# Attention and two MLPs: seven of the eight layer-in products formed as Strassen's seven block products

## The chip, the cores and the metric

The kernel runs on one core of a Trainium2 chip. A time is the device time of one launch in microseconds (us), and a kernel's time is the median of several runs. A profile is one execution taken by the hardware profiler. Its engines are PE (TensorE, matmuls), DVE (VectorE), ACT (ScalarE), POOL (GpSimd) and SP (which starts the DMA transfers). PE's weight loads are listed apart as PEld.

## The reference, cut to what matters

```python
# 2 batches, 8 heads, 1152 positions, head_dim 64
q_pool = q.reshape(B, H, S // 2, 2, D).mean(axis=3)
scores = np.matmul(q_pool, k.transpose(0, 1, 3, 2)) / np.sqrt(D)
attn = softmax(scores)                        # over the keys
x = np.matmul(attn, v)                        # -> (1152 tokens, 512)
h = x @ moe_w_in;  x = np.maximum(0.01 * h, h) @ moe_w_out
h = x @ moe2_w_in; x = (h / (1 + np.exp(-h))) @ moe2_w_out
```

`w_in` is 512 x 2048 and `w_out` 2048 x 512. The inputs come as 64-bit floats, which the kernel reads as pairs of 32-bit words and turns into fp32 itself.

## The kernel before

The program has two parts, `attention` (to about 212 us in the trace) and `mlps`. The change works in the second, and in the attention only where the two meet.

**Precision.** PE multiplies in fp32r. To reach fp32 accuracy each operand is held as a high part (rounded to fp32r) and a low part (what is left), and each product takes three matmuls: high by high, high by low, low by high. The tokens are held as `xh` and `xl`, the weights as `w0h`, `w0l` (layer-in) and `w1h`, `w1l` (layer-out), and what lies between the two products as `gh` and `gl`.

**Blocks, groups and cells.** Each MLP (called a layer here) is done in four blocks of 512 hidden columns, so there are eight blocks. The 1152 tokens are two groups: group 0 is one stretch of 512, group 1 two stretches of 320. A unit is a layer, a block and a group. `layer_in` (L1102) makes 128 hidden rows of a unit: four steps over the 512 model columns (`kk`), three matmuls each, one per stretch of tokens (L1115). So 256 hidden rows take 24 matmuls of 512 columns for group 0 and 48 of 320 for group 1. Layer 1 then applies Prelu twice on ACT (to `gh`, L1141, and to the full value `a`, L1146), layer 2 a Sigmoid on ACT (L1153), a multiply on DVE out of PSUM (L1157) and a copy on ACT (L1162). POOL subtracts to get `gl` (L1168).

`layer_out_t` (L1172, layer 1) and `layer_out` (L1223, layer 2) form the second product (L1186, L1244) and add it up over the blocks in `acc1` or `acc2` (DVE, L1207 and L1263). The last block of layer 1 also writes the tokens of layer 2 (`xh` L1213 on ACT, `xl` L1218 on POOL). Two units stand interleaved, the layer-in of one with the layer-out of the one before.

**Weights.** A piece is 128 x 512 weights, eight to a block. It is loaded by a DMA (L135), converted from 64-bit words in five steps (`convert_steps`, L158): an absolute value on ACT (L171), then four on DVE (L175 clamp, L179 shift, L183 sign, L188 tail), all in the SBUF tile `wt`. Two more steps split it, high on ACT (L206) and low on POOL (L210). Three tiles receive raw pieces and four hold converted ones.

**PSUM.** `Banks` (L91) hands out the eight banks in four pairs, in turn.

**The last pair of heads.** The attention's last normalization runs inside `mlps`, while PE is at the first unit: two reciprocals (L826), two multiplies (L827), the high part on ACT (L828) and the low part on DVE (L829), 288 columns each. Group 1 of block 0 needs them for its fourth step over `kk`.

**The order.** `Plan` (L228) is a list scheduler that runs while the program is built. Each task has an engine, an assumed duration, a due time, tasks it follows and buffers it takes and gives back. Of the tasks that are ready on an engine the one due first is written next. What it writes is a fixed order for each engine; on the chip an instruction waits only by its semaphores, and all behind it on its engine wait too.

Of the kernel before, what the change touches and what calls it, by code (L numbers as in the profile page):

```python
# [1341 lines left out]
```

## Time and profile before

| | |
|---|---|
| median of 3 runs | 619.52 us (618.24 to 620.22) |
| the profiled execution | 620.76 us |
| its span, first to last instruction | 618.8 us |
| mean granted TensorE clock | 0.986 of full speed |
| PE busy | 606.9 us, 98% of the span |
| DVE, ACT, POOL busy | 462.0, 292.2, 316.4 us |
| idle before PE's layer-in matmuls | 0.0 us in all three of its groups |

A share of busy time is an average over stages. The chain that ended last is what shows, for each stretch, which engine the end waited for. A group of instructions gives the mean duration of one, and a timeline a single one with what it waited for in brackets. [...] Rows of the timeline with "x2" stand for two instructions, and the length is that of both.

### The profile page before, as it was taken

To read this page: it belongs to the slowest core of one execution; us is meant where nothing else is said; L and a number is where in the kernel's file an instruction comes from. 1 tells how busy PE (TensorE), PEld (TensorE's weight loads), DVE (VectorE), ACT (ScalarE), POOL (GpSimd) and SP (SyncE) were. 2 spreads that over 40 slices of the span, in tenths; PEclk is the share of its full clock that TensorE was granted. 3 is DMA by queue.
4 is the path that set the end of the run, shared out by engine and by line. 5 is a ranking of instruction groups with operands and counts; after the bars stand their busy time and mean duration, and the time that the engine had idled before them with its cause. 6 is when DMAs were issued, how large, how long until landed. Compare 5 with 4: busy or idle time off the path is not lost.

```text
span 618.8 us, 10706 instructions
## 1 busy us (share of the span) xinstructions
PE 606.9 (98%) x4244; PEld 511.0 (83%) x4244; DVE 462.0 (75%) x588; ACT 292.2 (47%) x501; POOL 316.4 (51%) x224
## 2 busy tenths in 40 slices
PE   7998999999999999999999999999999999999997
PEld 5867677686687698899899899999988988988986
DVE  6799897797898999666677656989898978752122
ACT  4556566576476464454243433554555443432210
POOL 7857558466461066355364355766665544433120
PEclk9598999999999999999999999999999999999999
DMA  7122442454131123323223223223143332200012
GB/s 256 51 78 61 114 139 59 114 174 160 21 113 56 55 61 109 137 62 100 94 87 93 87 93 103 88 83 103 69 127 106 107 96 77 68 1 0 1 52 102
DMA packets 29529, 55.01 MB, mean 89 GB/s; under 512 B 13196, under 2 KB 14632, under 8 KB 29480
## 3 DMA queue, kind: packets, MB, share of 16 engines
q1 hardware_dynamic: 29336, 54.14, 27.7%
q8 instruction: 33, 0.54, 0.4%
q10 hardware_dynamic: 144, 0.20, 0.1%
q14 instruction: 16, 0.13, 0.1%
HBM read 49.81 MB, written 2.42 MB: 84 GB/s over the span
## 4 chain that ended last, share of the span: by engine, by line
PE 61%; DVE 4%; issue 0%; ACT 0%; POOL 0%
PE psum L1115 29%; PE psum L1244 16%; PE psum L1186 16%; DVE acc L714 1%; DVE r L826 1%; DVE wt L183 1%; DVE wt L188 1%; DVE xl L845 1%; DVE wt L175 0%; DVE wt L179 0%; DVE pvs L841 0%; ACT xh L844 0%; POOL w1l L210 0%; DVE xl L829 0%; DVE pvs L827 0%
## 5 line engine op out<-in xcount | busy, mean ns | idle before, releaser
L1168 POOL TENSOR_TENSOR gl<-a,gh 128x512 fp32r<-128x512 f32 (+1 forms) x64 | 99.6, 1559 | 104.5 <-ACT gh L1162 50.9
L1115 PE MATMUL psum<-xh,w0h 128*128 128x320 f32 (+1 forms) x384 | 108.7, 337 | 0.0
L1115 PE MATMUL psum<-xh,w0l 128*128 128x320 f32 (+1 forms) x384 | 108.6, 337 | 0.0
L1115 PE MATMUL psum<-xl,w0h 128*128 128x320 f32 (+1 forms) x384 | 108.5, 337 | 0.0
L676 ACT ACTIVATE e<-psum 128x512 f32<-128x512 f32 (+1 forms) x144 | 88.6, 664 | 20.8 <-PE psum L670 18.3
L548 DVE TENSOR_REDUCE mx<-psum 128x2 f32<-128x768 f32 x96 | 88.2, 950 | 12.1 <-PE psum L541 10.9
L210 POOL TENSOR_TENSOR w0l<-wt,w0h 128x512 fp32r<-128x512 f32 x32 | 42.6, 1333 | 75.0 <-ACT w0h L206 71.9
L175 DVE TENSOR_SCALAR wt<-wt 128x512 f32<-128x512 f32 x64 | 50.2, 785 | 37.7 <-ACT wt L171 37.7
L1115 PEld LDWEIGHTS psum<-xh,w0h 128*128 128x128 f32 x384 | 67.7, 188 | 7.5 <-issue 0.9
L728 PE MATMUL psum<-e,vnat 128*64 128x320 f32 (+1 forms) x576 | 72.5, 408 | 0.1
L1115 PEld LDWEIGHTS psum<-xh,w0l 128*128 128x128 f32 x384 | 66.8, 188 | 5.7 <-POOL w0l L210 0.3
L1115 PEld LDWEIGHTS psum<-xl,w0h 128*128 128x128 f32 x384 | 66.8, 188 | 5.0
L210 POOL TENSOR_TENSOR w1l<-wt,w1h 128x512 fp32r<-128x512 f32 x32 | 44.7, 1395 | 38.1 <-ACT w1h L206 38.1
L179 DVE TENSOR_SCALAR wt<-wt 128x512 uint32<-128x512 uint32 x64 | 62.6, 979 | 1.6
L728 PEld LDWEIGHTS psum<-e,vnat 128*64 128x64 f32 x576 | 40.3, 137 | 28.3 <-ACT e L676 1.4
L714 DVE TENSOR_TENSOR acc<-acc,e 128x512 f32<-128x512 f32 (+1 forms) x77 | 62.5, 847 | 0.9
L183 DVE SCALAR_TENSOR_TENSOR wt<-wraw,wt 128x512 uint32<-128x512 uint32 x64 | 61.4, 960 | 1.6
L714 POOL TENSOR_TENSOR acc<-acc,e 128x512 f32<-128x512 f32 (+1 forms) x35 | 49.7, 1420 | 21.1 <-DVE acc L714 13.8
L188 DVE SCALAR_TENSOR_TENSOR wt<-wraw,wt 128x512 uint32<-128x512 uint32 x64 | 57.2, 893 | 1.8
L1244 PE MATMUL psum<-w1l,gh 128*128 128x512 f32 (+1 forms) x148 | 56.9, 385 | 0.0
L1244 PE MATMUL psum<-w1h,gh 128*128 128x512 f32 (+1 forms) x148 | 56.9, 385 | 0.0
L1244 PE MATMUL psum<-w1h,gl 128*128 128x512 f32 (+1 forms) x148 | 56.8, 384 | 0.0
(86 smaller groups left out, 1137.2 us busy)
## 6 DMA issues: line engine op xcount, KB each, us to landing
wraw<-in_moe_w_in_dram SPq DMA_DIRECT2D x32, 512.0 KB, 4.7
wraw<-in_moe_w_out_dram SPq DMA_DIRECT2D x32, 512.0 KB, 3.2
vnat<-in_v_dram SPq DMA_DIRECT2D x8, 576.0 KB, 6.5
knat<-in_k_dram SPq DMA_DIRECT2D x7, 576.0 KB, 6.2
qnat<-in_q_dram SPq DMA_DIRECT2D x7, 576.0 KB
out_dram<-acc SPq DMA_DIRECT2D x8, 256.0 KB, 2.0
xl<-pvs SPq DMA_DIRECT2D x7, 288.0 KB, 4.8
xh<-d SPq DMA_DIRECT2D x14, 144.0 KB, 2.9
```

Of the source, the lines that this page charges most:

```text
L179: nc.vector.tensor_scalar(out=t, in0=t, scalar1=4, scalar2=1, op0=ALU.logical_shift_left, op1=ALU.logical_shift_right)
L183: nc.vector.scalar_tensor_tensor(out=t, in0=box["high"], scalar=0x80000000, in1=t, op0=ALU.bitwise_and, op1=ALU.bitwise_or)
L188: nc.vector.scalar_tensor_tensor(out=box["out"], in0=box["low"], scalar=29, in1=box["t"], op0=ALU.logical_shift_right, op1=ALU.bitwise_or)
L210: self.nc.gpsimd.tensor_tensor(out=lo, in0=tf, in1=hi, op=ALU.subtract)
L548: nc.vector.tensor_reduce(out=mx[p][:, u, c], in_=ps[:, :, 0:KC], op=ALU.max, axis=AX.X)
L676: nc.scalar.activation(out=e_t[h, t], in_=ps[:, :, 0:n], func=ACTF.Exp, scale=scale)
L714: e.tensor_tensor(out=a, in0=e_t[h, 0] if t == 1 else a, in1=e_t[h, t], op=ALU.add)
L728: nc.tensor.matmul(out=vps[h][0][own[j], 0, 0:CW[c]], lhsT=vnat[p][:, j, t, :], rhs=e_t[h, t][:, j, :], start=(t == 0), stop=(t == NKT - 1),)
L1115: nc.tensor.matmul(out=box[x][:, c, 0:n], lhsT=wt[:, kk, fs], rhs=m[:, kk, chunk(g, c)], start=(kk == 0 and wt is wh and m is xh), stop=(k ...
L1168: nc.gpsimd.tensor_tensor(out=gl, in0=box["a", x], in1=gh, op=ALU.subtract)
L1186: nc.tensor.matmul(out=box[x][:, c, 0:n], lhsT=wt[:, f, ms], rhs=y[:, c * n:(c + 1) * n], start=(f == 0 and wt is oh and y is gh), stop=(f ...
L1244: nc.tensor.matmul(out=box[x][:, c, 0:n], lhsT=y[:, ts], rhs=wt[:, f, cs], start=(f == 0 and y is gh and wt is oh), stop=(f == FB - 1 and ...
```

## The change

Block 0 of layer 1 keeps its layer-in. For the other seven blocks the layer-in of 256 hidden rows and one group of tokens, a cell in what follows (28 of them), is taken as a product of 2 x 2 matrices of blocks: the 512 model columns in two halves, the 256 hidden rows in two halves of 128, the tokens of the group in two halves (256 or 320). Strassen's method, in Winograd's form, needs seven block products M1 to M7 instead of eight, each of 2 steps over `kk` by three matmuls: 42 matmuls of 256 or 320 columns.

It needs sums of the operands:

- *Tokens.* T1 to T4 are differences of token blocks, four subtractions on DVE for each layer and group (`transform`), each with a high part on ACT and a low part on POOL (the last two of layer 2's group 1 on DVE). For layer 1 the full tokens are first rebuilt from `xh` and `xl` on DVE (`rebuild`, L1207, four for each group).
- *Weights.* Each layer-in piece keeps three of its 128-column parts, copied by ACT, and gets four sums on DVE (`combine`). The split then runs over seven parts, 896 columns, instead of 512. Its DMA fetches two stretches of 512 words for each row instead of one of 1024.
- *Results.* The products of a cell lie in two PSUM pairs. ACT copies M1 out (e1), and DVE forms eu, ev, c1 and c2. M2 is written into M1's bank, M3 into M6's and M4 into M7's, so they follow e1, eu and ev. Prelu and Sigmoid then read SBUF.

The weight conversion of `mlps` runs in one PSUM pair that it keeps, one bank to a piece, and three pairs are left for matmuls. Raw pieces have two tiles instead of three, converted ones three instead of four. SiLU's multiply moves from DVE to POOL. A unit's layer-out now stands between its successor's two halves.

```diff
+    transform=10.0,
+    more=3.0,
     conv=4,
     early=3,
     early_due=60.21,
     split=4,
-    wt=4,
+    wt=3,
+    raw=2,
...
-        if kind == 0:
-            src = w[i * 128:(i + 1) * 128, 2 * fb * n:2 * (fb + 1) * n]
+        t = self.raw_p.tile([128, 2 * n], U32, tag="raw", name="wraw")
+        to = t
+        if kind == 1:
+            src = w[fb * n + i * 128:fb * n + (i + 1) * 128, :]
+        elif blk == 0:
+            src = w[i * 128:(i + 1) * 128, 0:2 * n]
         else:
-            src = w[fb * n + i * 128:fb * n + (i + 1) * 128, :]
-        t = self.raw_p.tile([128, src.shape[1]], U32, tag="raw", name="wraw")
-        self.nc.sync.dma_start(out=t, in_=src)
+            c = 2 * fb * n + (i // 2) * n
+            src = w[:, c:c + n].rearrange("(b k p) c -> k p b c", b=2, p=128)[i % 2]
+            to = t.rearrange("p (b c) -> p b c", b=2)
+        self.nc.sync.dma_start(out=to, in_=src)
...
+            if psum:
+                box["tf"] = psum(box["n"])
...
+        def copy():
+            new()
+            nc.scalar.activation(out=self.mid[box["n"]][:, 0:384], in_=box["tf"][:, 0:384], func=ACTF.Copy)
+        def sums():
+            self.combine(box["n"], box["tf"])
+        return (begin, clamp, shift, sign, tail) + ((copy, sums) if parts else ())
+    def combine(self, n, raw):
+        v = self.mid[n].rearrange("p (m f) -> p m f", f=128)
+        a12, _, a11, a21 = (raw[:, 128 * m:128 * (m + 1)] for m in range(4))
+        for to, x, y, op in (
+            (4, a21, v[:, 1], ALU.add), (5, v[:, 2], a21, ALU.subtract), (6, v[:, 4], a11, ALU.subtract), (3, a12, v[:, 6], ALU.subtract)
+        ):
+            self.nc.vector.tensor_tensor(out=v[:, to], in0=x, in1=y, op=op)
...
+            parts = [self.slots[self.SLOTS[i]][:, 896 * x:896 * (x + 1)] for x in range(2)]
+            self.tiles[blk, kind, i] = [x.rearrange("p (m f) -> p m f", f=128) for x in parts]
...
+    conv_ps, _ = banks.take()
...
+        if ph in (2 * NBLK - 1, 2 * NBLK):
+            order += outs + ins
+        elif ph == 2 * NBLK + 1:
+            order += ins + outs
+        else:
+            order += ins[0:1] + outs + ins[1:2]
...
+            steps = weights.convert_steps(lambda n: conv_ps[:, n % 2, :], kind == 0)
+            costs = ("ACT", 0.62), ("DVE", 0.62), ("DVE", 0.65), ("DVE", 0.65), ("DVE", 0.69), ("ACT", 0.5), ("DVE", 0.9)
+            into, last = (5, 6) if kind == 0 else (4, 4)
...
+        t1 = step(lo2(0), lo2(1), lo2(0), after, 0)
+        t3 = step(lo2(1), lo1(1), lo2(1), [t1], 2)
+        t2 = step(lo1(1), lo1(1), lo2(0), [t1, t3], 1)
+        t4 = step(lo1(0), lo1(0), lo1(1), [t2], 3)
...
+            fast = layer == 1 and g == 1 and m > 1
...
+    def rebuild(g, after):
+        made = []
+        for k in range(KDM):
+            made.append(add(
+                "DVE", 0.07 + 2 * groups[g][1] / 860, P["transform"] - 1.0 + 18.0 * g,
+                lambda k=k: nc.vector.tensor_tensor(
+                    out=acc1[:, k, both(g)], in0=xh[:, k, both(g)].bitcast(F32), in1=xl[:, k, both(g)].bitcast(F32), op=ALU.add
+                ),
+                after=after,
+            ))
...
+                "POOL", wp, d, lambda: nc.gpsimd.tensor_tensor(out=a(), in0=a(), in1=box["t", u, f], op=ALU.mult),
...
+    PRODUCTS = dict(M1=(2, "B11"), M2=(0, "B21"), M3=(3, "B22"), M4=(1, "T4"), M5=(4, "T1"), M6=(6, "T2"), M7=(5, "T3"))
...
+        place = dict(M1=(kx, 0), M6=(kx, 1), M5=(ky, 1), M7=(ky, 0), M2=(kx, 0), M3=(kx, 1), M4=(ky, 0))
+        weight = [split_t[b, 0, 2 * fp + kk] for kk in range(2)]
+        def product(m):
+            key, bank = place[m]
+            i, name = PRODUCTS[m]
+            if m in ("M1", "M5"):
+                take(key)
+            for kk in range(2):
+                wh, wl = weights.tiles[b, 0, 2 * fp + kk]
+                bh, bl = operand(name, g, kk)
+                for q, (w, y) in enumerate(((wh, bh), (wh, bl), (wl, bh))):
                     nc.tensor.matmul(
-                        out=box[x][:, c, 0:n],
-                        lhsT=wt[:, kk, fs],
-                        rhs=m[:, kk, chunk(g, c)],
-                        start=(kk == 0 and wt is wh and m is xh),
-                        stop=(kk == KDM - 1 and wt is wl),
+                        out=box[key][:, bank, 0:n], lhsT=w[:, i, :], rhs=y,
+                        start=(kk == 0 and q == 0), stop=(kk == 1 and q == 2),
...
+        m1 = pe("M1")
+        e1 = add(
+            "ACT", 0.18 + n * 0.84e-3, d, lambda: nc.scalar.activation(out=part(0), in_=ps(kx, 0), func=ACTF.Copy),
+            after=[m1] + end_made, take=("sc",),
+        )
+        m6 = pe("M6")
+        eu = add("DVE", wp, d, lambda: vadd(part(3), ps(kx, 1), part(0)), after=[m6, e1])
+        m5, m7 = pe("M5"), pe("M7")
+        ev = add("DVE", wp2, d, lambda: vadd(part(1, 3), ps(ky, 0, 2), part(3).broadcast_to([128, 2, n])), after=[m5, m7, eu])
+        m2, m3, m4 = pe("M2", [e1]), pe("M3", [eu]), pe("M4", [ev])
+        e1 = add("DVE", wp2, d, c1, after=[m2, m3, ev], take=("ac",), give=("duo",))
+        e2 = add("DVE", wp2, d, c2, after=[m4], order=[e1], give=("duo", "sc"))
```

PE, one layer-in after a layer-out of group 1 of layer 1, before (each line is a matmul with its operands and columns):

```order
L1115 MATMUL psum<-xh,w0h 128x512
L1115 MATMUL psum<-xl,w0h 128x512
L1115 MATMUL psum<-xh,w0l 128x512
L1115 MATMUL psum<-xh,w0h 128x512
L1115 MATMUL psum<-xl,w0h 128x512
L1115 MATMUL psum<-xh,w0l 128x512
```

PE, the first cell, in the changed order; `more` holds the weights' seven parts, `th` and `tl` the token differences:

```order
L1329 MATMUL psum<-xh,more 128x256
L1329 MATMUL psum<-xl,more 128x256
L1329 MATMUL psum<-xh,more 128x256 x2
L1329 MATMUL psum<-xl,more 128x256
L1329 MATMUL psum<-xh,more 128x256
L1329 MATMUL psum<-th,more 128x256
L1329 MATMUL psum<-tl,more 128x256
L1329 MATMUL psum<-th,more 128x256 x2
L1329 MATMUL psum<-tl,more 128x256
L1329 MATMUL psum<-th,more 128x256
```

The matmuls have 256 columns instead of 512, a cell has 42 instead of 24, and some of their operands are the new differences.

DVE at the last pair's normalization, before (L175 to L188 are a weight piece, L826 to L829 the last pair, L845 another pair):

```order
L845 TENSOR_TENSOR xl<-pvs,xh 128x576
L175 TENSOR_SCALAR wt<-wt 128x512
L179 TENSOR_SCALAR wt<-wt 128x512
L183 SCALAR_TENSOR_TENSOR wt<-wraw,wt 128x512
L188 SCALAR_TENSOR_TENSOR wt<-wraw,wt 128x512
L826 RECIPROCAL r<-r 128x288 x2
L827 TENSOR_TENSOR pvs<-pvs,r 128x288 x2
L175 TENSOR_SCALAR wt<-wt 128x512
L829 TENSOR_TENSOR xl<-pvs,xh 128x288 x2
```

The same place after the change; L1207 is the rebuilding of the tokens, L184 to L199 the conversion, L851 to L854 the last pair:

```order
L877 TENSOR_TENSOR xl<-late,xh 128x576
L1207 TENSOR_TENSOR acc_2680<-xh,xl 128x512 x2
L184 TENSOR_SCALAR psum<-psum 128x512 x2
L188 TENSOR_SCALAR psum<-psum 128x512 x2
L192 SCALAR_TENSOR_TENSOR psum<-wraw,psum 128x512 x2
L199 SCALAR_TENSOR_TENSOR wt<-wraw,psum 128x512 x2
L1207 TENSOR_TENSOR acc_2680<-xh,xl 128x512 x2
L851 RECIPROCAL late<-late 128x288 x2
L852 TENSOR_TENSOR late<-late 128x288 x2
L184 TENSOR_SCALAR psum<-psum 128x512
L854 TENSOR_TENSOR xl<-late,xh 128x288 x2
```

Four rebuilds and eight conversion steps now stand between the other pair's L877 and the reciprocals, where four conversion steps stood.

DVE behind the last add of layer 1 (L1207 of before), before:

```order
L1207 TENSOR_TENSOR acc_2723<-psum,acc_2723 128x640
L179 TENSOR_SCALAR wt<-wt 128x512
L183 SCALAR_TENSOR_TENSOR wt<-wraw,wt 128x512
L188 SCALAR_TENSOR_TENSOR wt<-wraw,wt 128x512
L1157 TENSOR_TENSOR a<-psum,t 128x512
L175 TENSOR_SCALAR wt<-wt 128x512
L179 TENSOR_SCALAR wt<-wt 128x512
L1157 TENSOR_TENSOR a<-psum,t 128x512
L183 SCALAR_TENSOR_TENSOR wt<-wraw,wt 128x512
L188 SCALAR_TENSOR_TENSOR wt<-wraw,wt 128x512
```

The same place after the change: the last add is L1417, and it, L184, L188 and the first cell's eu (L1351 of 128x256) stand just ahead of these rows; L1351 is the combining of a cell, L1173 and L1193 the token differences of layer 2's group 1:

```order
L192 SCALAR_TENSOR_TENSOR psum<-wraw,psum 128x512
L1351 TENSOR_TENSOR late<-psum,late 128x512
L199 SCALAR_TENSOR_TENSOR wt<-wraw,psum 128x512
L1351 TENSOR_TENSOR late<-psum,late 128x512
L1173 TENSOR_TENSOR acc_2680<-acc_2680 128x2x320
L1351 TENSOR_TENSOR late<-psum,late 128x512
L1173 TENSOR_TENSOR acc_2680<-acc_2680 128x2x320
L184 TENSOR_SCALAR psum<-psum 128x512
L1173 TENSOR_TENSOR acc_2680<-acc_2680 128x2x320
L1193 TENSOR_TENSOR xl<-acc_2680,xh 128x2x320
L1173 TENSOR_TENSOR acc_2680<-acc_2680 128x2x320
L1351 TENSOR_TENSOR late<-psum,late 128x256
```

Before, the first operation that a layer-in of layer 2 needs stands behind three conversion steps. Now the last row is eu of the second cell; counted from the last add it stands behind four combines of the first cell, five operations on the tokens and five conversion steps.

## Rows read from the trace of the kernel before

**Rows 1.** The page's part 1: busy us of each engine, share, instructions.

```profile
PE 606.9 (98%) x4244; PEld 511.0 (83%) x4244; DVE 462.0 (75%) x588; ACT 292.2 (47%) x501; POOL 316.4 (51%) x224
```

**Rows 2.** The chain that ended last: start, length, engine, tile, line, count.

```profile
237.43 1.76 PE psum L1115 x12
...
276.91 7.04 PE psum L1115 x48
...
407.81 14.07 PE psum L1186 x96
...
587.42 2.74 PE psum L1244 x12
```

**Rows 3.** PE's timeline at the end of the program: start, length, instruction.

```profile
612.60 0.28 PE L1244 MATMUL psum<-w1h,gh 128*128 128x256 f32 x1
...
615.35 0.28 PE L1244 MATMUL psum<-w1h,gl 128*128 128x256 f32 x1
```

**Rows 4.** Busy time by stretch: PE, PEld, DVE, ACT, POOL; PEclk, DMA share, GB/s.

```profile
49.00:52.50 3.50, 3.50 (x34) 3.50 (x32) 2.96 (x4) 1.69 (x3) 0.63 (x2) 0.51 0.37 130
450.00:500.00 50.00, 50.00 (x254) 43.41 (x253) 43.87 (x52) 26.06 (x45) 27.20 (x20) 1.00 0.34 110
```

**Rows 5.** DVE's timeline at the start of the MLPs.

```profile
217.77 0.42 DVE L175 TENSOR_SCALAR wt<-wt 128x512 f32<-128x512 f32 x1
...
218.69 0.69 DVE L183 SCALAR_TENSOR_TENSOR wt<-wraw,wt 128x512 uint32<-128x512 uint32 x1
219.41 1.67 DVE L188 SCALAR_TENSOR_TENSOR wt<-wraw,wt 128x512 uint32<-128x512 uint32 x1
221.00 3.75 DVE L826 RECIPROCAL r<-r 128x288 f32<-128x288 f32 x2
...
225.69 0.82 DVE L829 TENSOR_TENSOR xl<-pvs,xh 128x288 fp32r<-128x288 f32 x2
```

**Rows 6.** DVE groups by line and shape: busy, mean ns; idle before, releaser.

```profile
L179 DVE TENSOR_SCALAR wt<-wt 128x512 uint32<-128x512 uint32 x64 | 62.6, 979 | 1.6
...
L183 DVE SCALAR_TENSOR_TENSOR wt<-wraw,wt 128x512 uint32<-128x512 uint32 x64 | 61.4, 960 | 1.6
...
L188 DVE SCALAR_TENSOR_TENSOR wt<-wraw,wt 128x512 uint32<-128x512 uint32 x64 | 57.2, 893 | 1.8
...
L175 DVE TENSOR_SCALAR wt<-wt 128x512 f32<-128x512 f32 x64 | 50.2, 785 | 37.7 <-ACT wt L171 37.7
...
L1263 DVE TENSOR_TENSOR acc<-psum,acc 128x512 f32<-128x512 f32 x26 | 17.9, 689 | 27.9 <-PE psum L1244 27.9
...
L1157 DVE TENSOR_TENSOR a<-psum,t 128x640 f32<-128x640 f32 x16 | 13.1, 820 | 15.7 <-ACT t L1153 15.7
...
L1263 DVE TENSOR_TENSOR acc<-psum,acc 128x256 f32<-128x256 f32 x2 | 0.8, 425 | 1.8 <-PE psum L1244 1.8
```

**Rows 7.** POOL groups of the same view.

```profile
L1168 POOL TENSOR_TENSOR gl<-a,gh 128x640 fp32r<-128x640 f32 x32 | 54.0, 1688 | 49.2 <-ACT gh L1162 29.3 <-ACT a L1146 19.2 <-POOL xl L1218 0.7
...
L1168 POOL TENSOR_TENSOR gl<-a,gh 128x512 fp32r<-128x512 f32 x32 | 45.6, 1430 | 55.3 <-ACT a L1146 29.9 <-ACT gh L1162 21.6 <-PE psum L1115 3.7
...
L210 POOL TENSOR_TENSOR w1l<-wt,w1h 128x512 fp32r<-128x512 f32 x32 | 44.7, 1395 | 38.1 <-ACT w1h L206 38.1
```

**Rows 8.** The page's part 6: DMA issues, KB each, us to landing.

```profile
wraw<-in_moe_w_in_dram SPq DMA_DIRECT2D x32, 512.0 KB, 4.7
```

**Rows 9.** PE's timeline where group 1 begins.

```profile
224.82 0.45 PE L1115 MATMUL psum<-xh,w0h 128*128 128x320 f32 x2
...
227.46 0.46 PE L1115 MATMUL psum<-xh,w0h 128*128 128x320 f32 x2
```

**Rows 10.** PE's timeline in the attention.

```profile
48.38 0.69 PE L765 MATMUL psum<-acc,ones 128*32 128x288 f32 x8 [1.67 <-DVE acc L714]
```

**Rows 11.** PE's timeline at the first layer-out.

```profile
235.58 0.50 PE L1186 MATMUL psum<-gh,w1h 128*128 128x512 f32 x1 [0.40 <-ACT w1h L206]
...
236.93 0.50 PE L1186 MATMUL psum<-gh,w1l 128*128 128x512 f32 x1 [0.63 <-POOL w1l L210]
```

More of the change, by code (lines that the diff above doesn't have):

```diff
@@ L809, in pe @@
         def pe():
-            box["end"] = banks.turn()
+            box["end"], box["end i"] = banks.take()
             for c in range(2):
@@ L1061, in weight_tasks @@
         for n in range(P["split"], len(pieces)):
-            d = piece_due(n)
+            blk, kind, i = pieces[n]
+            d = first[pieces[n]] - P["ahead"] - P["more"] * (kind == 0)
             x = []
@@ L1066, in weight_tasks @@
                 x = [load]
-            if n >= wt0:
-                weigh = (("ACT", 0.66), ("DVE", 0.8), ("DVE", 1.1), ("DVE", 0.75), ("DVE", 0.75))
-                for m, (step, (eng, w)) in enumerate(zip(weights.convert_steps(), weigh)):
-                    x = [add(
-                        eng, w, d, step, after=x, order=[conv] if m == 0 and conv else [],
-                        take=(("wt", n),) if m == 0 else (), give=(("raw", n),) if m == 4 else (),
-                    )]
-                conv = x[0]
@@ L1075, in weight_tasks @@
-            high, low = weights.split_steps()
-            hi = add("ACT", 0.62, d, high, after=x, order=[hi] if hi else [])
-            lo = add("POOL", 1.45, d, low, after=[hi], give=(("wt", n),))
-            late.append((hi, pieces[n]))
-            split_t[n] = [hi, lo]
-    weight_tasks()
-    def split_of(blk, kind, i):
-        return split_t[pieces.index((blk, kind, i))]
-    def matmuls(x, tiles, deps, take, part=1.0, before=()):
-        kind, (layer, blk, g), i = x
-        w = part * 3 * (0.227 if g == 0 or (kind == "out" and layer == 1) else 0.292)
-        made = list(before)
-        for k in range(FB):
-            t = add(
-                "PE", w, due[x], lambda k=k: tiles(k), after=deps(k), order=made[-1:],
-                take=(take,) if k == 0 and take else (), lag=0.25,
-            )
-            made.append(t)
-            users.setdefault((layer * NBLK + blk, int(kind == "out")), []).append(t)
-        return made
@@ new lines, in weight_tasks @@
+            steps = weights.convert_steps(lambda n: conv_ps[:, n % 2, :], kind == 0)
+            costs = ("ACT", 0.62), ("DVE", 0.62), ("DVE", 0.65), ("DVE", 0.65), ("DVE", 0.69), ("ACT", 0.5), ("DVE", 0.9)
+            into, last = (5, 6) if kind == 0 else (4, 4)
+            for m, (step, (eng, w)) in enumerate(zip(steps, costs)):
+                x = [add(
+                    eng, w, d, step, after=x, order=[conv] if m == 0 and conv else [],
+                    take=(("cv", n),) * (m == 0) + (("wt", n),) * (m == into),
+                    give=(("raw", n),) * (m == 4) + (("cv", n),) * (m == last),
+                )]
+                conv = x[0] if m == 0 else conv
@@ new lines, in weight_tasks, with used, chain @@
+            high, low = weights.split_steps()
+            w = 7 / 4 if kind == 0 else 1.0
+            hi = add("ACT", 0.1 + 0.5 * w, d, high, after=x, order=[hi] if hi else [])
+            lo = add("POOL", 0.1 + 1.3 * w, d, low, after=[hi], give=(("wt", n),))
+            highs[pieces[n]] = hi
+            split_t[pieces[n]] = [hi, lo]
+    weight_tasks()
+    def used(b, kind, i, t):
+        users.setdefault((b, kind, i), []).append(t)
+    def chain(x, steps):
+        made = []
+        for w, go, after, take in steps:
+            made.append(add("PE", w, due[x], go, after=after, order=made[-1:], take=take, lag=0.25))
+        return made
@@ L1275, in pair_end @@
         pe, act, steps = end()
-        t = add("PE", 1.2, P["end"], pe, take=(("p", "end"),), begin=P["end"])
-        t = add("ACT", 0.65, P["end"], act, after=[t], give=(("p", "end"),))
+        t = add("PE", 1.2, P["end"], pe, take=("duo",), begin=P["end"])
+        t = add("ACT", 0.65, P["end"], act, after=[t], give=("duo",))
         made = []
```

508 lines of the change are left out of this document (314 added, 194 removed).

## The prediction

> **What bounds the kernel now.** I read the page's busy line first: PE works 606.9 of 618.8 us [rows 1]. Then the chain of waits from its end backwards: from 237.43 on every step is PE, `layer_in` (L1115) in turn with `layer_out` (L1186, then L1244) [rows 2]. From there to the end no engine is waited for, and the time is matmuls times columns. The same rows give the rates: 12 matmuls of 512 columns in 2.74 us, .228 each; 48 of 320 in 7.04, .147 each. The 24 matmuls of 256 columns at the end start 2.75 us apart over 23 gaps [rows 3]: .120 each. So the rate per column holds at the changed kernel's sizes, and the saving on PE can be counted. What the other engines have in reserve decides how much of it stays: DVE is busy 43.9 of 50 us in layer 2 [rows 4].
>
> **Matmuls removed: -18.7 us.** There are 28 cells (seven blocks, two groups, two halves). Group 0: 24 of 512 columns become 42 of 256, 24 x .2283 = 5.48 against 42 x .1196 = 5.02, .46 less, x14 = 6.4. Group 1: 48 of 320 become 42, 7.04 against 42 x .1467 = 6.16, .88 less, x14 = 12.3. `layer_out` keeps its count.
>
> **A DVE step in PSUM.** No row shows the conversion there, so its price decides the rest. Bounds: .42, the first step alone in SBUF [rows 5], and .98, the dearest of the four means today (.785, .979, .960, .893, together 3.62 a piece [rows 6]). I take .69, the nearest row that reads PSUM at this width (L1263, the mean of 26 [rows 6]; POOL is busy 27.2 of 50 us in that layer [rows 4]).
> Alone, an SBUF step with two inputs takes .69 and, with POOL at work on another piece, 1.67 [rows 5]. [...]
>
> **DVE per block, as a check of cover.** Sums of 128 columns: 256 cost .425 and 512 .689 [rows 6], so an estimate of .29 (at most .425). Layer 1: conversion 8 x 4 x .69 = 22.1; sums 16 x .29 = 4.7; combines of four cells 2 x (.425 + 3 x .69) + 2 x (.49 + 3 x .82) = 10.9, .82 from L1157; adds after `layer_out` 4 x .69 + 4 x .82 = 6.0. Together 43.7. PE per block: cells 10.0 + 12.3, out 48 x .228 = 10.9 and 14.1 [rows 2], 47.3. Layer 2: 43.8 against 47.0. DVE keeps up on average with 8% to spare: no bound, but it will be late wherever work bunches.
> POOL in layer 2 now also multiplies: 4 x 1.43 + 4 x 1.69 [rows 7] = 12.5, twice (multiply and lows) 25.0, weight lows 4 x 1.40 and 4 of 896 columns. From 1.43 at 512 and 1.69 at 640 those come to 2.2 (between 1.69 and two of 512, 2.86): 14.4. Sum 39.4 of 47.0. ACT gains 61 instructions and was busy 47% [rows 1]: covered. With two raw buffers a new piece is needed every 5.9 us (47.3 / 8), so each has 11.8; landing 4.7 [rows 8] and four steps, 2.8, fit.
>
> **Start of the MLPs: +4.2.** Ahead of the last pair's reciprocals DVE now does four conversion steps, 217.77 to 221.00 = 3.2 [rows 5]. In the changed order four rebuilds (L1207) and eight PSUM steps stand there, 12 x .69 = 8.3, 5.1 more; and between multiply and `xl` a step in PSUM in place of one of .42, .3 more. `xl`, done at 225.69 + .82 = 226.5, comes at 231.9. PE needs it in the second matmul of the fourth k of group 1, .29 after 227.46 [rows 9]: 4.2 late. It is in order: nothing behind passes. Bounds 1.7 (conversion steps at .42) and 6.7 (at .98).
> **Clock: +1.75.** [...]
> **First cell: +1.0.** Its pieces are 896 wide on ACT and POOL and come right after the late DVE work; they arrive about when PE does. Bounds 0 and 2.9, a whole POOL low.
> **Waits of today: -1.0.** .40 on ACT and .63 on POOL [rows 11] fall away or lie in the shadow of the longer one.
>
> **Change of layers: +2.7 and +.9.** From the last add of layer 1 to the second cell's first combine (eu) the DVE order has the add .82, five conversion steps 3.45, the first cell's four combines 2.5, five transforms of group 1 4.1 and eu itself .43: 11.3. PE reaches the product that wants it after one cell and five products, 5.02 + 5 x .72 = 8.6. So +2.7 (0 to 6, from steps at .42 to .98 with transforms held up by POOL). [...]
> [...]
>
> **Inside the cells: +2.8.** The fourth product wants eu, two products after its inputs: some .45 us (group 0) or .6 (group 1) of slack behind the combine. When a conversion step of .69 has just begun, it is missed by up to .25. I take .1 per cell, x28; bounds 0 and .3 (8.4).
>
> **Sum:** -18.7 + 4.2 + 1.75 + 1.0 - 1.0 + 2.7 + .9 + 2.8 = -6.35. The profiled execution took 620.76, so 614.4; it stands 1.2 above the median of the runs, 619.52, and against that the forecast is 613.2.
>
> **Rivals.**
> *A, the forecast:* 609 to 617.5, the bounds of start, layer change and cells taken partly together. Chance .46.
> *B, the waits are covered:* PSUM steps nearer .42 to .6, so that DVE is early everywhere. For it: the bare .42 [rows 5]; against it: the rows that read PSUM at 512 columns take .69. Only the matmuls and a few us of the start count: -18.7 - 1.0 + 1.7 for the start and up to 6 left of clock, cells and layer change: 602 to 608. Chance .23.
> *C, the waits double:* between my values and the upper bounds lie 2.5 (start), 1.9 (first cell), 3.3 (layer change), 5.6 (cells) and 2.6 (clock); and in layer 2 multiply and low, 1.69 each on POOL with ACT's copy between, now both stand ahead of `layer_out`. If 4.5 to 8.2 of this comes, 617.7 to 621.4, no change. For it: one engine in fixed order between PE's products; against it: 8% to spare. Chance .15.
> *D, DVE becomes the bound (slower):* if a PSUM step takes more than .80, 43.7 + 32 x (s - .69) exceeds 47.3 in each Strassen block, and PE runs at DVE's rate. Every .01 above costs .32 us a block, 1.92 over six (the last has no weights to convert for a next); the gain of 6.35 is used up at .833. At .87 the time is 613.2 + 13.4 = 627, at .95 it is 642. For it: three of today's four steps average .89 to .98 beside POOL. Against it: L1263's .69 with POOL at work. Range 622 to 642, chance .16.
> That fewer matmuls are not issued after all is excluded: the order has 588 of 256 and 588 of 320 columns, 42 in each of 28 cells.
>
> **How the numbers follow.** Less than 0.3% (617.7 to 621.4) can't be told from no change. Faster: A and B, .69; same: C, .15; slower: D, .16. The likeliest is A, 613.2, its own range 609 to 617.5. Eight in ten: from B's fast end at 602 to the first part of D, 624; what lies outside, some .03 below and .13 above, is the end of B and most of D.
>
> **What would show it.** PE busy about 590 (606.9 - 18.7 + slow stretches). The mean of the conversion steps: .69 for A, under .6 for B, over .8 for D. A gap on PE near 227.5 of about 4 us with `xl` (DVE) as releaser, and a granted clock near .5 behind it. A second gap of 2 to 3 us at the second cell of layer 2. In a stretch of layer 1, PE's share near full for A, DVE's instead for D. I am wrong if L1329's wait in the middle of layer 1 is on DVE all the time, if the start's wait stays under 2 us, or if POOL's lows release most matmuls of layer 2.

## The result, and the profile after

The changed kernel is slower by .6%: 621.37 us, the median of 18 runs, against 618.23 in 18 runs of the kernel before beside it. The ratio is 1.0056, 95% interval 1.0035 to 1.0076. The forecast was 613.2 against a median of 619.52: 6.35 us less were expected, 3.1 more came.

The profiled execution took 619.83 us, one of the quicker of its kind, that of before 620.76, one of the slower. So I compare the MLPs alone, from the first layer-in matmul to the last add: 212.30 to 615.66 before, 403.4 us; 207.93 to 614.93 after, 407.0. That is 3.6 us more, about what the medians say. (The attention, whose PE work is unchanged, took 4 us less in this execution, at a granted clock of .93 instead of .85 in its first 50 us.)

PE's busy time fell from 606.9 us [rows 1]. From the page's part 1 after:

```profile
PE 591.2 (96%) x4412; PEld 506.3 (82%) x4412; DVE 510.3 (83%) x808; ACT 336.9 (55%) x573; POOL 391.6 (63%) x268
```

In the middle of a layer the saving is all there. In the chain of waits after (start, length, engine, tile, line, count) these two pieces stand one block apart:

```profile
324.19 11.13 PE psum L1329 x84
...
371.35 5.00 PE psum L1329 x42
```

371.35 - 324.19 = 47.16 us; the prediction had 47.3. PE's own timeline has no wait over 0.1 us between them. Nearly all that was lost lies at two places, the start of the MLPs and the change of layers. All waits of PE over 0.1 us in the MLPs (start, length, instruction, in brackets the idle time ahead and what ended it):

```profile
211.16 0.73 PE L1283 MATMUL psum<-xh,w 128*128 128x512 f32 x2 [0.39 <-POOL w L231]
...
226.84 0.99 PE L1283 MATMUL psum<-xh,w 128*128 128x320 f32 x2 [2.96 <-ACT xh L853]
...
244.83 5.49 PE L1398 MATMUL psum<-g,wout 128*128 128x512 f32 x12 [3.40 <-ACT acc L1415]
...
265.32 11.71 PE L1398 MATMUL psum<-g,wout 128*128 128x320 f32 x78 [0.26 <-DVE late L1351]
...
401.02 0.41 PE L1329 MATMUL psum<-xh,w 128*128 128x320 f32 x1 [2.00 <-DVE late L1351]
...
403.88 0.42 PE L1329 MATMUL psum<-th,w 128*128 128x320 f32 x1 [0.85 <-DVE late L1351]
...
405.53 6.72 PE L1398 MATMUL psum<-g,wout 128*128 128x320 f32 x44 [0.50 <-DVE a L1351]
...
412.42 6.13 PE L1398 MATMUL psum<-g,wout 128*128 128x320 f32 x40 [0.17 <-POOL g L1235]
...
426.85 0.41 PE L1329 MATMUL psum<-xh,more 128*128 128x320 f32 x1 [0.57 <-DVE late L1351]
...
433.90 0.58 PE L1329 MATMUL psum<-xh,w 128*128 128x256 f32 x1 [5.20 <-DVE late L1351]
...
605.38 9.52 PE L1464 MATMUL psum<-wout,g 128*128 128x512 f32 x52 [0.24 <-DVE g L1235]
```

The two long ones at the start are 6.4 us, the five over .4 at the change of layers 9.1, and the four short ones (.39, .26, .17, .24) 1.1. Before there were 1.0 us [rows 11]. Three of the gaps are followed by slow matmuls: 12 of 512 columns take 5.49 us behind 244.83, where 2.74 is the full rate [rows 2]. By stretch (PE, PEld, DVE, ACT, POOL; granted clock, DMA share, GB/s):

```profile
212.00:265.00 53.00, 46.65 (x247) 40.55 (x245) 48.10 (x75) 29.96 (x53) 33.54 (x21) 0.90 0.26 78
265.00:387.00 122.00, 121.74 (x793) 115.99 (x793) 100.10 (x179) 64.65 (x108) 68.49 (x46) 1.00 0.29 92
387.00:434.00 47.00, 37.65 (x261) 35.89 (x259) 45.10 (x64) 27.83 (x46) 37.32 (x25) 0.97 0.22 68
434.00:449.00 15.00, 15.00 (x91) 15.00 (x92) 13.03 (x22) 7.41 (x14) 12.61 (x10) 0.85 0.24 69
```

The slow clock costs 1.8 us behind 226.84 (ten matmuls of 320 columns in 3.25 us instead of 1.47), 2.75 behind 244.83 and 15 x .15 = 2.25 from 434 on: an estimate of 6.8. So 16.5 of waits and 6.8 of clock, less the 1.0 of before, are 22.3 against 18.7 saved: 3.6 worse, as measured. The clock's part belongs to this one execution: over the 18 runs the mean granted clock was .970 to .989, here .981.

The DVE groups (busy, mean ns; idle before, releaser):

```profile
L188 DVE TENSOR_SCALAR psum<-psum 128x512 uint32<-128x512 uint32 x60 | 41.5, 694 | 0.9
L184 DVE TENSOR_SCALAR psum<-psum 128x512 f32<-128x512 f32 x60 | 41.4, 691 | 10.3 <-ACT psum L180 10.1
L192 DVE SCALAR_TENSOR_TENSOR psum<-wraw,psum 128x512 uint32<-128x512 uint32 x60 | 41.4, 691 | 1.1
...
L219 DVE TENSOR_TENSOR wt<-psum,wt 128x128 f32<-128x128 f32 x56 | 16.1, 288 | 6.3 <-ACT wt L205 5.3
...
L1173 DVE TENSOR_TENSOR acc<-acc 128x512 f32<-128x512 f32 x8 | 11.8, 1479 | 0.0
...
L1173 DVE TENSOR_TENSOR acc<-acc 128x640 f32<-128x640 f32 x8 | 11.3, 1410 | 0.0
```

The conversion steps take the .69 that was forecast, with POOL at work, and the sums .29. The token subtractions, L1173, take 1.41 us on average for 640 columns, where .82 was forecast. DVE's timeline ahead of the longest gap shows how:

```profile
423.38 2.81 DVE L1173 TENSOR_TENSOR acc<-acc 128x640 f32<-128x640 f32 x1
...
426.72 0.81 DVE L1173 TENSOR_TENSOR acc<-acc 128x640 f32<-128x640 f32 x1
...
428.05 1.58 DVE L1173 TENSOR_TENSOR acc<-acc 128x640 f32<-128x640 f32 x1
429.56 1.89 DVE L1193 TENSOR_TENSOR xl<-acc,xh 128x640 fp32r<-128x640 f32 x1
431.37 2.15 DVE L1173 TENSOR_TENSOR acc<-acc 128x640 f32<-128x640 f32 x1
433.44 0.41 DVE L1351 TENSOR_TENSOR late<-psum,late 128x256 f32<-128x256 f32 x1
```

POOL's in the same stretch:

```profile
422.96 2.55 POOL L231 TENSOR_TENSOR wout<-wt,wout 128x512 fp32r<-128x512 f32 x2
427.04 1.91 POOL L1193 TENSOR_TENSOR tl<-acc,th 128x640 fp32r<-128x640 f32 x1 [1.53 <-ACT th L1187]
428.91 1.85 POOL L1259 TENSOR_TENSOR late<-late 128x512 f32<-128x512 f32 x1
430.73 2.11 POOL L1193 TENSOR_TENSOR tl<-acc,th 128x640 fp32r<-128x640 f32 x1
```

POOL's end at 428.95, 430.76 and 432.84; DVE's end at 429.63, 431.45 and 433.52, .68 or .69 later each time. A DVE operation with both inputs in SBUF that comes while POOL works ends here about .68 after POOL's instruction, however long that is (after two of them at 423.38); begun with POOL idle, at 426.72, it took .81. eu (the last DVE row), for which PE has stood since 428.7, comes right behind. From 418.59, the last add of layer 1, to eu DVE was never idle, so the gap is made of DVE's own time and not of waits for POOL's results.

### The profile page after: what moved, and what is told of

Its sections match the earlier page's. It is cut to its first block, busy times and chain, and to the rows that moved or that the text cites. A ratio compares the mean times of both kernels' runs of the same rounds, so it can differ in the third digit from the quotient of the medians.

```text
span 618.0 us, 11491 instructions
## 1 busy us (share of the span) xinstructions
PE 591.2 (96%) x4412; PEld 506.3 (82%) x4412; DVE 510.3 (83%) x808; ACT 336.9 (55%) x573; POOL 391.6 (63%) x268
## 4 chain that ended last, share of the span: by engine, by line
PE 76%; DVE 12%; ACT 5%; issue 4%; POOL 2%; DMA 1%; SPq 0%; DVEq 0%; POOLq 0%; ACTq 0%
PE psum L1329 23%; PE psum L1464 15%; PE psum L1398 14%; PE psum L693 12%; PE psum L751 7%; PE psum L564 3%; DVE acc L1173 3%; DVE late L737 2%; ACT e L699 1%; DVE mx L571 1%; DVE acc L1207 1%; PE psum L596 1%; DVE late L1351 1%; DMA qnat<-in_q_dram 1%; PE psum L789 1%
## 5 line engine op out<-in xcount | busy, mean ns | idle before, releaser
L1398 PE MATMUL psum<-g,wout 128*128 128x320 f32 (+1 forms) x576 | 106.0, 342 | 4.3 <-ACT acc L1415 3.4
L1398 PEld LDWEIGHTS psum<-g,wout 128*128 128x128 f32 x576 | 93.8, 191 | 13.3 <-ACT acc L1415 3.8
L1464 PE MATMUL psum<-wout,g 128*128 128x512 f32 (+1 forms) x444 | 100.7, 384 | 0.3 <-DVE g L1235 0.2
L1464 PEld LDWEIGHTS psum<-wout,g 128*128 128x128 f32 x444 | 81.1, 188 | 16.7 <-DVE g L1235 0.7
L1351 DVE TENSOR_TENSOR late<-psum,late 128x256 f32<-128x256 f32 (+3 forms) x84 | 54.5, 653 | 21.4 <-PE psum L1329 18.9
L737 DVE TENSOR_TENSOR late<-late,e 128x512 f32<-128x512 f32 (+1 forms) x77 | 63.7, 862 | 0.9
L737 POOL TENSOR_TENSOR late<-late,e 128x512 f32<-128x512 f32 (+1 forms) x35 | 49.9, 1425 | 21.1 <-DVE late L737 13.8
L1329 PE MATMUL psum<-xh,w 128*128 128x256 f32 (+1 forms) x224 | 50.8, 300 | 7.3 <-DVE late L1351 7.2
L693 PE MATMUL psum<-qh,kh 64*128 64x320 f32 (+1 forms) x288 | 49.6, 341 | 1.3 <-DVE mx L571 0.5
L1329 PE MATMUL psum<-xh,more 128*128 128x256 f32 (+1 forms) x224 | 49.7, 294 | 0.6 <-DVE late L1351 0.6
L184 DVE TENSOR_SCALAR psum<-psum 128x512 f32<-128x512 f32 x60 | 41.4, 691 | 10.3 <-ACT psum L180 10.1
```

The lines of the kernel that those rows point to most:

```text
L184: nc.vector.tensor_scalar(out=tf, in0=tf, scalar1=2.0, scalar2=W_TOP, op0=ALU.max, op1=ALU.min)
L693: nc.tensor.matmul(out=ps[:, j, 0:n], lhsT=lhsT[own[j], :], rhs=rhs[own[j], cs], start=m == 0, stop=m == len(terms) - 1)
L737: e.tensor_tensor(out=a, in0=e_t[h, 0] if t == 1 else a, in1=e_t[h, t], op=ALU.add)
L1329: nc.tensor.matmul(out=box[key][:, bank, 0:n], lhsT=w[:, i, :], rhs=y, start=(kk == 0 and q == 0), stop=(kk == 1 and q == 2),)
L1351: nc.vector.tensor_tensor(out=to, in0=p, in1=y, op=ALU.add)
L1398: nc.tensor.matmul(out=box[x][:, c, 0:n], lhsT=wt[:, ms], rhs=y[:, c * n:(c + 1) * n], start=(f == 0 and y is gh and wt is oh), stop=(f == ...
```

## Experiments

The first three take away one suspected cost each and keep every engine's order as it was in the changed kernel. Ratios are to the kernel before, run beside each (the changed kernel: 1.0056).

**d1: the subtractions made small.**

```diff
-nc.vector.tensor_tensor(out=to, in0=x, in1=y, op=ALU.subtract)
+nc.vector.tensor_tensor(out=to[:, :, 0:32], in0=x[:, :, 0:32], in1=y[:, :, 0:32], op=ALU.subtract)
```

> The changed kernel, but each of the sixteen token subtractions (transform) works on 32 columns of each half instead of 256 or 320; the rest of the differences is left out, so the output isn't the reference's. Order of every engine as in the changed kernel. Theory (the waits come from the token subtractions on DVE, 0.7 to 2.8 us each, at the start and at the change of layers): the waits of 2.0, 0.85 and 5.2 us around 401 to 434 us fall to 1 us together and the one of 3.4 at 244 shrinks to under 1.5, with their slow clock; 621.4 falls by 12 to 16, to 606 to 609. Rival (the eight conversion steps and the combines make DVE late, the subtractions only stand in the same place): more than half of the waits stays, 615 or more.

613.70 us, ratio .992 (.9892 to .9948): 8 us better than the changed kernel, less than the theory's 12 to 16 and more than the rival allows. The wait at the second cell only went from 5.20 to 3.98. The reason is in its rows (all such instructions; then some of them, DVE's and POOL's):

```profile
L1174 DVE TENSOR_TENSOR acc<-acc x16: 207/942/2209, 232.4 to 424.8; 128x64 f32<-128x64 f32 x16
```

```profile
418.03 2.21 DVE L1174 TENSOR_TENSOR acc<-acc 128x64 f32<-128x64 f32 x1
420.76 0.21 DVE L1174 TENSOR_TENSOR acc<-acc 128x64 f32<-128x64 f32 x1
...
424.80 1.55 DVE L1174 TENSOR_TENSOR acc<-acc 128x64 f32<-128x64 f32 x1
```

```profile
417.60 2.56 POOL L231 TENSOR_TENSOR wout<-wt,wout 128x512 fp32r<-128x512 f32 x2
...
424.15 2.12 POOL L1194 TENSOR_TENSOR tl<-acc,th 128x640 fp32r<-128x640 f32 x1
```

An operation of 64 columns takes .21 us with POOL idle, and 2.21 or 1.55 where POOL works until 420.16 and 426.27. There its own size hardly matters; it buys a place behind POOL's instruction. So d1 did not take the suspected cost away at this place. At the start it did: counted from the first matmul of the MLPs, the tile that waited 3.40 starts after 35.3 us (243.92 - 208.64) instead of 36.9.

**d2: POOL's work made small.** The same cut stands at the other lows and multiplies named below.

```diff
+cut = slice(0, 64) if u in ((0, NBLK - 1, 0), (0, NBLK - 1, 1), (1, 0, 0)) else slice(None)
-(nc.vector if fast else nc.gpsimd).tensor_tensor(out=gl, in0=a(), in1=gh, op=ALU.subtract)
+(nc.vector if fast else nc.gpsimd).tensor_tensor(out=gl[:, cut], in0=a()[:, cut], in1=gh[:, cut], op=ALU.subtract)
```

> The changed kernel, but POOL's operations around the change of layers (weight lows of block 4, gl of layer 1's last block and of layer 2's first unit of group 0, token lows of layer 2, the first multiplies) work on 64 columns instead of 512 to 896; what they leave out is stale, so the output isn't the reference's. Theory (a DVE operation with both inputs in SBUF is held up by POOL's): the eight subtractions there fall from 1.4 to 2.8 us to 0.7 to 0.8 each, the wait of 5.2 at the second cell of layer 2 to 0.5 to 2.7, in all 5 to 8 us less than 621.4: 613 to 616. Rival (they are slow by themselves, both inputs and the output in one tile): means stay above 1.3, the gap stays within 1 us of 5.2, 620 to 622.

611.73 us, ratio .9886 (.9831 to .9941), better than the theory's 613 to 616. The eight subtractions, of full size here, and the wait at the second cell (minimum, median, maximum ns; then PE's timeline):

```profile
L1176 DVE TENSOR_TENSOR acc<-acc x8: 682/750/943, 397.5 to 427.1; 128x512 f32<-128x512 f32 x4, 128x640 f32<-128x640 f32 x4
```

```profile
428.43 0.58 PE L1336 MATMUL psum<-xh,w 128*128 128x256 f32 x1 [2.22 <-DVE late L1358]
```

The waits before it, in layer 1's last cells, are gone. So 3.0 of the 5.2 us are POOL's doing. The other 2.2 are the order itself, which the prediction priced at 2.7; but DVE now stands 1.15 us waiting for ACT (.50 at 424.28, .65 at 426.35), which the prediction did not have, so that the two numbers are close in part by luck. The start, which this edit leaves alone, was quicker too in this execution: the fourth layer-out tile starts 36.9 us after the first matmul, as in the changed kernel, but PE comes there later, behind a longer slow stretch (twenty matmuls of 320 columns in 5.83 us from 230.98 on, where the changed kernel has ten in 3.25), waits less and loses no clock behind it. In v1 and v2, whose orders are those of the changed kernel up to 381 us, the wait is shorter too and no clock is lost (d2, v1, v2):

```profile
248.88 3.01 PE L1405 MATMUL psum<-g,wout 128*128 128x512 f32 x12 [2.07 <-ACT acc L1422]
```

```profile
245.88 3.06 PE L1412 MATMUL psum<-g,wout 128*128 128x512 f32 x12 [2.33 <-ACT acc L1429]
```

```profile
248.20 3.03 PE L1412 MATMUL psum<-g,wout 128*128 128x512 f32 x12 [2.20 <-ACT acc L1429]
```

From the first matmul to the one at 265.32 the changed kernel's trace takes 57.4 us and these three 56.0, 55.4 and 56.5: 1 to 2 us of what their traces gained on it belong to the execution and not to the edit.

**d3: the gaps filled.** One layer-out tile is also issued twice.

```diff
+again = {((0, NBLK - 1, 1), 1): 3, ((1, 0, 0), 1): 7}.get((u, fp), 0)
...
+for _ in range(again):
+    m2 = add("PE", 0.0, due[x], lambda: product("M2"), order=[m2], lag=0.25)
...
```

> The changed kernel with matmuls done twice where PE waits: the third layer-out tile of the first unit (2.7 us before the wait of 3.4), the fifth product three times more in layer 1's last cell (2.6 us before the wait of 2.0) and seven times more in the second cell of layer 2 (5.0 us before the wait of 5.2). Order of the other engines as in the changed kernel. Theory (each gap is followed by a stretch at the lower clock, which is lost on top of the wait): the granted clock stays near 1.00 behind the two filled places, 2.5 to 2.8 us come back at the first and 2.2 at the second: 616 to 617.5 instead of 621.4. Rival (the slow matmuls are hidden by the next DVE wait): within 1 us of 621.4.

619.30 us, ratio 1.0004 (.9971 to 1.0037): 2.1 us less by the medians where 4 to 5.4 were expected, and the two intervals touch. The clock stayed up (387 to 450: granted 1.00 instead of .95):

```profile
387.00:450.00 63.00, 60.14 (x416) 57.87 (x416) 59.89 (x88) 38.00 (x64) 52.34 (x34) 1.00 0.21 68
```

and behind the first place twelve matmuls take 3.01 us, not 5.49. That alone says little, since in d2, v1 and v2 they take 3.01 to 3.06 with the gap unfilled. PE, sooner there, waits again for DVE and ACT (.74 at 259.57, .79 at 435.91). So a gap's slow clock is a part of the loss, in part hidden by the next wait; how large a part, this run does not settle.

**v1: the first block of each layer plain.** Six blocks in seven products instead of seven.

```diff
-    plain = lambda u: u[0:2] == (0, 0)
+    plain = lambda u: u[1] == 0
```

(with the loads, the SiLU out of PSUM and the readiness of the tokens made to fit, and layer 2's token subtractions due later).

> The first block of layer 2 is plain too, as that of layer 1 (six of eight blocks in seven products); its multiply then reads PSUM on DVE. The token subtractions of layer 2 may then lie beside some 25 us of plain matmuls. Theory (the loss at the change of layers is DVE's lateness with the subtractions in front of a cell's first combine): waits of 9.3 us and 2.3 of slow clock go, 2.7 us of the saving are given back: 621.4 - 8.9 = 612.5 (610 to 615). Rival (the subtractions then hold up the layer-out of that block, whose accumulator shares their memory): the waits move to the layer-out, 619 or more.

614.20 us, ratio .994 (.9909 to .997): as the theory had it, 7 us better than the changed kernel though 2.7 of the saving are given back. No wait is left in layer 2's first block. Group 0's subtractions still stand in layer 1's last unit:

```profile
399.58 0.41 PE L1343 MATMUL psum<-xh,w 128*128 128x320 f32 x1 [1.42 <-DVE late L1365]
401.60 0.63 PE L1343 MATMUL psum<-th,w 128*128 128x320 f32 x1 [0.88 <-DVE late L1365]
```

**v2 and v5: later still.** On v1: layer 2's subtractions wait for layer 1's last cell. With `box["x", 1]` in place of `x_read[0, 1][-1:]` (v5, which also has the start of v4) they wait for its last add.

```diff
+after = after + (x_read[0, 1][-1:] if u[0] else [])
 transformed[u[2]] = transform(u[0], u[2], after, plain_read[u[0], u[2]])
```

> v1_plain_each with the token subtractions of layer 2 put behind the last cell of layer 1. Theory: in v1 they still stood in front of a cell's combine in layer 1's last unit (three of them 4.67 us) and cost waits of 1.42 and 0.88 us and 1.7 us of slow clock; all of it goes, 614.2 - 4 = 610 (609 to 611.5). Rival (pushed later they hold up the first layer-out of layer 2, whose accumulator shares their memory): a wait of over 2 us there, 613 or more.

> v4_pool_rebuild with all token subtractions of layer 2 put behind the last add of layer 1. Theory: in v4 (as in v2) group 0's subtractions stand ahead of the adds that free PSUM pairs, PE waits 2.15 us for L1431 and loses 1.9 at the lower clock; both go: 611.9 - 4 = 608 (606.5 to 609.5). Rival (there is no free place: they then hold up the multiplies out of PSUM in layer 2's first unit or its layer-out): a wait of 2 us or more after 415, 611 or more.

v2: 614.26 us, ratio .9932 (.9906 to .9957). v5: 612.46 us, ratio .9885 (.9845 to .9924), as v4. The rivals were right both times in time and size, v2's not in the place: its wait came in the last layer-out of layer 1 (L1412). The wait moves with the subtractions. v2, then v5:

```profile
412.85 7.36 PE L1412 MATMUL psum<-g,wout 128*128 128x320 f32 x38 [2.15 <-DVE acc L1431]
```

```profile
447.98 7.16 PE L1477 MATMUL psum<-wout,g 128*128 128x512 f32 x24 [2.43 <-DVE a L1264]
```

**v3, v4 and s1: the start.** On v2: v3 has the first edit, v4 the other two as well; s1 is the changed kernel, seven blocks in seven products, with v4's start alone.

```diff
-t = add("PE", 1.2, P["end"], pe, take=("duo",), begin=P["end"])
+t = add("PE", 1.2, -20.0, pe, take=("duo",), begin=P["end"])
... (the steps behind it on ACT and DVE likewise)
-"DVE", 0.07 + 2 * groups[g][1] / 860, P["transform"] - 1.0 + 18.0 * g,
+"DVE" if g else "POOL", 0.07 + 2 * groups[g][1] / (860 if g else 435), P["transform"] - 1.0 + 18.0 * g,
... (the engine in its lambda likewise)
-rebuild(u[2], end_made * u[2])
+rebuild(u[2], (end_made + transformed[0][-2:-1]) if u[2] else [])
```

> v2_later with the last pair's sums and normalization due first on PE, ACT and DVE. Theory (DVE is the bound of the whole start, its work until group 0's subtractions are done is the same): the wait of 3.3 us before group 1's fourth step goes, but PE comes sooner to the fourth layer-out tile and waits there for what it saved, 2.3 us become 4 to 6; 0 to 2 less than v2_later, 608 to 610. Rival (the wait was one of order alone): both together fall under 2.5 us, 605 to 606.

> v3_end_first with group 0's tokens rebuilt on POOL (idle some 4 us there) and group 1's behind group 0's subtractions. Theory (DVE's work ahead of group 0's subtractions is what PE waits for; 3.7 us of it go to POOL, 4.6 behind): the waits of 3.3 and 2.3 us and their slow clock shrink to under 1.5 together, 602 to 605. Rival (POOL's four operations of both inputs in SBUF hold up DVE's normalization of pairs, which PE needs first): 608 or more.

> The changed kernel (seven blocks in seven products) with the start of v4_pool_rebuild alone: the last pair's normalization first, group 0's tokens rebuilt on POOL, group 1's behind group 0's subtractions. Theory: the start's waits of 2.96 and 3.40 us and 4.3 us of slow clock become some 6 us of short waits without slow clock, as in v4: 621.4 - 4 = 617 (615.5 to 619); the waits at the change of layers stay. Rival (the start follows the change of layers in importance, nothing to gain by itself): 620 or more.

v3: 619.54 us, ratio 1.0011 (.9985 to 1.0037), 5 us worse than v2 and outside both its ranges. The wait of 2.9 us shrinks to .64 and 1.03, and another of 4.71 (for `a`, L1249, from ACT) comes in at 240.87, with a clock of .90 in 212 to 265. v4: 611.89 us, ratio .9886 (.9851 to .9922), 2 to 3 better than v2, 602 to 605 expected; in the two traces, from the first layer-in matmul to the last add, the MLPs take 398.6 and 399.6 us, 1.0 less. s1: 622.11 us, ratio 1.0077 (1.0052 to 1.0102), nothing gained, as its rival had it (the MLPs take 406.6 us instead of 407.0). In v4 and s1 the waits are for the second half of `w_out`, converted behind what was put first; s1's, then v4's, at the same place:

```profile
244.81 6.22 PE L1398 MATMUL psum<-g,wout 128*128 128x512 f32 x19 [2.52 <-POOL wout L231]
```

```profile
244.52 4.61 PE L1412 MATMUL psum<-g,wout 128*128 128x512 f32 x19 [0.92 <-POOL wout L231]
```

The 21 matmuls ahead of this wait take 6.68 us in v4, at a granted clock of .76 (236.9 to 244), and 5.06 in s1, at 1.00; the 19 behind it 4.61 in v4, at 1.00, and 6.22 in s1, at .59 (244.8 to 249). The slow stretch fell ahead of the wait in v4 and was hidden by it, and behind it in s1. So the two rows differ by the clock of one execution each, and in these traces the edit gains little in either kernel: the start is short of DVE and POOL work time, and an order only chooses who waits.

**v7: group 0's subtractions on POOL,** in layer 2, on top of v5.

```diff
+pool = layer == 1 and g == 0
-"DVE", w, d + 0.1 * m, lambda: nc.vector.tensor_tensor(out=to, in0=x, in1=y, op=ALU.subtract), after=deps
+"POOL" if pool else "DVE", 0.13 + 2 * n / 440 if pool else w, d + 0.1 * m,
+lambda: (nc.gpsimd if pool else nc.vector).tensor_tensor(out=to, in0=x, in1=y, op=ALU.subtract), after=deps
```

> v5_after_last_add with the four token subtractions of layer 2's group 0 on POOL, where their lows are already. Theory (DVE loses to POOL with both inputs in SBUF; on one engine they can't hold each other up): the wait of 2.43 us on L1264 in layer 2's first block and 1.5 us at the lower clock go, 612.2 - 3 to 4 = 608.5 to 609.5. Rival (POOL, busy 51 of 63 us there, becomes late with the lows of layer 2's first unit): a wait on POOL of 2 us or more, 612 or more.

611.57 us, ratio .9916 (.9887 to .9946): no better than v4 and v5. The wait on L1264 is gone, one of 1.87 us on POOL's `wout` low comes at 443.10, nearer the rival.

**e8: the conversion in PSUM alone,** all blocks plain, on the kernel before.

```diff
+conv_ps, _ = banks.take()
-for name, n in (("p", 4), ("t", 2), ("a", 2), ("raw", 3), ("wt", P["wt"])):
+for name, n in (("p", 3), ("t", 2), ("a", 2), ("raw", 3), ("wt", P["wt"]), ("cv", 2)):
...
-for m, (step, (eng, w)) in enumerate(zip(weights.convert_steps(), weigh)):
+for m, (step, (eng, w)) in enumerate(zip(weights.convert_steps(lambda: conv_ps[:, next(turns) % 2, :]), weigh)):
...
```

> The kernel before with one part of the change alone: the weight conversion of the MLPs in a PSUM pair of its own, three pairs left for matmuls, all blocks plain. Theory: the four conversion steps take .69 each whatever POOL does (2.8 us a piece instead of 3.6), DVE's busy time falls by some 45 us, and the time stays, since PE was never waiting: 617 to 621. Rival (three pairs are too few for plain blocks): waits of PE on evacuations in each block, 623 or more.

615.78 us, ratio .9939 (.9911 to .9966), a little faster than the 617 to 621 expected. The steps:

```profile
L175 DVE TENSOR_SCALAR psum<-psum 128x512 f32<-128x512 f32 x60 | 41.6, 694 | 37.0 <-ACT psum L171 37.0
```

DVE is busy 410 us instead of 462 and PE has no wait at all in the MLPs, where 1.0 us stood before. That explains 1.0 of the 3.1 us between the medians. In the two traces the MLPs take 401.6 us (210.49 to 612.13) against 403.4, 1.7 less; the other 1.8 between these two executions lie ahead of the MLPs, where kernels with an unchanged attention differed by 4 us (above), and whether e8 causes them isn't shown.

By itself this part of the change is worth as much as v1 (.994). So measured against e8, what else is changed gains nothing clear of noise in v1, 3.3 us in v5, which ran beside e8 (612.46 against 615.78), and costs 5.6 in the changed kernel (621.37).

## Why the prediction was wrong

- *The matmuls, -18.7:* right. A block takes 47.16 us where 47.3 was worked out.
- *A conversion step in PSUM, .69:* right, .69 for all of them (means of .682 to .694 over the 240 in PSUM, POOL busy for 63% of the span), and so rival D (a step over .80) was not what made it slower. One reading of [rows 5] is not right: POOL was at a unit's `gl`, not at another piece, and the step of .69 called alone ran beside it. It began .04 us ahead of POOL, which then took 1.80 us instead of the 1.28 of the same operation at 223.34:

```profile
218.73 1.80 POOL L1168 TENSOR_TENSOR gl<-a,gh 128x512 fp32r<-128x512 f32 x1 [3.80 <-ACT a L1146]
```

- *Change of layers, +2.7 and +.9:* the step that failed. It priced the five token operations at .82, from a row with one input in PSUM (L1157, [rows 6]). They have both inputs in SBUF, and the row for that stood in [rows 5]: .69 where it began ahead of POOL, 1.67 where POOL was ahead. In the trace they took .81 to 2.81, together 9.2 us instead of 4.1. The bound of 6 named it ("transforms held up by POOL"), the value did not use it. From the last add to the end of eu DVE took 15.3 us, not 11.3; PE came to its product after 10.1, not 8.6. Besides, group 0's four subtractions stand ahead of the combines of layer 1's last cells and were not in the sum. Together 9.1 us of waits, not 2.7. Shown by d2 (POOL's part, 3.0 of 5.2 and the earlier waits) and v1 (the place).
- *Start, +4.2 and first cell, +1.0:* the wait for the last pair came, 2.96, for `xh` from ACT and not for `xl`; the twelve DVE operations took the 8.3 us worked out (213.94 to 222.24). The first cell waited for nothing. The 3.40 at 244.83 was not seen: the fourth layer-out tile needs a PSUM pair, the copy that frees it writes the tile that the subtractions and their lows still read:

```profile
244.18 1.57 ACT L1415 ACTIVATE acc<-psum 128x512 f32<-128x512 f32 x3 [3.64 <-POOL tl L1193]
```

d1 shows it: with small subtractions the tile starts 1.6 us sooner. A cure was not found (s1).
- *Clock, +1.75 and +.9:* a slow clock came behind the three long gaps (granted .50 from 226.84 to 230.09 and from 244.80 to 250.30, .85 from 434 to 449), but no run shows 1.75 or .9 at these places. The execution of the changed kernel lost an estimated 6.8: 1.8 behind the gap of 2.96 us, 2.75 behind 3.40 and 2.25 behind 5.20. The kernel before shows 1.7 elsewhere: 3.5 us at .51 [rows 4], behind an idle 1.67 [rows 10]. Not every gap had one behind it: 2.07, 2.20 and 2.33 us ahead of the fourth layer-out tile cost none in d2, v2 and v1 (granted clock 1.00 behind them; twelve matmuls in 3.01, 3.03 and 3.06 us), 2.15 and 2.43 elsewhere in v2 and v5 did cost one (.76 and .78 in the 7 us behind).
- *Inside the cells, +2.8:* too much. From 265 to 387 us there is one wait over .1, of .26, and from 449 on one, of .24.

With 9.1 for 2.7, 6.4 for 5.2, 6.8 for 2.65 and 1.1 of short waits for 2.8 the sum is the 3.6 worked out above, to rounding. Rival C (the waits double, up to 621.4) came nearest, and more waiting at the same seams is what happened. That its time fits is in part luck: the change of layers and the clock went past its bounds (6.4 and 4.15 above the forecast, where it had 3.3 and 2.6), and the 5.6 that it kept for the cells did not come.

## What to carry to other kernels

Price a VectorE operation by its operands. Here a 512-column conversion step in PSUM took .69 us with GpSimd idle (L184 at 390.14) and with GpSimd at work (at 410.60); a subtraction with both inputs in SBUF took .81 us for 640 columns begun with GpSimd idle and 1.58 to 2.81 beside it. An average load of 92% says nothing on the places where all work changes at once; list what stands there ahead of the instruction that PE waits for, each at its price beside GpSimd. And a saving that is steady in the middle of a program can be lost at two seams: leaving the seam on the plain method (v1, v4: 612 to 614 us, better than both kernels) was worth more than its share of the saving. Measure each part of a change by itself, too: the step that only made room for the new method (e8, 615.8 us) gave about half of what the best of these kernels gained.

## What the runs showed of the hardware

A VectorE subtraction of 64 columns, .21 us alone, took up to 2.21 us behind two GpSimd instructions in a row. GpSimd pays too: in the changed kernel its single 512-column operations around both seams take 1.27 to 1.32 us where VectorE works from PSUM (at 223.44 on a reciprocal), and 1.73 to 1.88 where a VectorE operation with both inputs in SBUF began first.
